# Causal mask and identity from a band read back from DRAM, with the head's steps in another order

## The chip, the cores and the metric

The kernel runs on one core of one Trainium2 chip. A core has five engines that run their own instruction streams side by side: TensorE (PE, matrix products; its weight loads are counted apart as PEld), VectorE (DVE), ScalarE (ACT), GpSimd (POOL) and SyncE (SP, which here only issues DMAs). Streams meet at semaphores. Data lies in DRAM, in SBUF (128 partitions) and in PSUM (the accumulators that PE writes).

The metric is device microseconds of one execution. Three runs of the kernel before took 962.62, 963.16 and 964.15 us (median 963.16).

## The reference, cut to what matters

```python
def _attn_ref(q, k, v, f_logit):             # 4 batches, 8 heads, 768 tokens, 48 features
    f = 1.0 / (1.0 + np.exp(-f_logit))
    state = zeros(B, H, D, D)
    for t in range(S):
        state = f[:, :, t, :, None] * state + einsum('bhd,bhe->bhde', k[:, :, t], v[:, :, t])
        y[:, :, t] = einsum('bhd,bhde->bhe', q[:, :, t], state)
    return y

def _moe_ref(x, w_in, w_out):                # 3072 tokens, 384 -> 2048 -> 384
    h = x @ w_in
    return (softplus(h) @ w_out)

def _moe2_ref(x, w_in, w_out):
    h = x @ w_in
    return (h * tanh(softplus(h))) @ w_out

def reference(**kwargs):
    x = heads_joined(_attn_ref(...))         # 3072 tokens x 384
    return _moe2_ref(x=_moe_ref(x=x, ...), ...)
```

The output is the second MLP's.

## The kernel before, in words

**Recurrence.** The 768 tokens of a batch are cut into 6 chunks of 128; a pair (chunk, batch) is a group, 24 in all, numbered by chunk first. Within a group the recurrence is written in closed form: running products of the decays (a scan on DVE, `a_scan`), their inverses (two ACT activations, `a_inv`), q and k scaled by them (`a_q`, `a_k` on DVE), all scores of a head pair at once on PE (`a_scores`), a causal mask on them (`a_mask`, two DVE products with `mask`, a 128x128 tile of ones on and above the diagonal), and the masked scores times v (`a_out`, `a_rest`). Eight heads of 48 features lie as four pairs. The outputs come feature first, in blocks of 48 rows, and must stand in x as three blocks of 128; so `a_out` makes the first rows of the pairs, `a_outed` copies them from PSUM on ACT (letter O), and `a_rest` puts them into place by a product with a 0/1 matrix `sel` (L407) and adds the other heads' rows (L411); `a_rested` copies the sum to x on ACT (letter R). `ident` is the 128x128 identity; `a_turn` needs it to transpose k for the states of the next chunk, and `sel` is filled with pieces of it.

**MLPs.** Layers 1 and 2 are cut into 6 blocks of 512 tokens by 16 blocks of 128 hidden features, 192 units in all. A unit is a product into the hidden block (L467 in the plain float32 units at the start, L481 later), the activation function (ACT and DVE), and a product out of it (L601, L611). The input weights arrive as float64 and are taken apart by integer operations on DVE and ACT: letters A (`whole_a`, DVE), B (`whole_b`, ACT L171) and C (`whole_c`, DVE L176 and L187) for a weight block.

**What sets the order around the change.** SP issues the first loads in the order of the table `LOADS`: f (decay logits), k (q and k together), v of a group, w a weight block. The steps ahead of the first unit are written out in the table `HEAD`, a letter and a group (or weight block) each, and are issued in that order on ACT, DVE, PE and SP; every engine runs its own share of them in the order of the table, so a step that waits holds up all steps of its engine behind it. Letters not named so far: e is exp of the logits on ACT, P and p add 1 on DVE or on ACT, s the scan, i the inverses, q and k the products, S the scores, m both masks, o and y the first rows of the outputs, b the rest of them, t T x X turns and states, h a number of matmuls without use (`warm`). After the head, units below 80 are ordered by the scheduler of the framework under hooks, and later ones by hand.

POOL makes `ident` and `mask` in the kernel before, by affine_select (through the helper `make_identity` at L742, and at L752), and fills `sel` from `ident` (L748); the matmuls of `warm` multiply `ident` by itself.

Of the kernel before, what the change touches and what calls it, by code (L numbers as in the profile page):

```python
# [8 lines left out]

F32 = mybir.dt.float32  # L10
F32R = mybir.dt.float32r
# [3 lines left out]
ALU = mybir.AluOpType  # L15
PSUM = bass.MemoryType.PSUM

B, H, S, D = 4, 8, 768, 48
C = 128
# [5 lines left out]
KD = DM // 128  # L25
N = B * C
R = 112
CAP = 2.0 ** 60
SAFE = 2.0 ** 40
# units are (layer, block of 512 tokens, block of 128 hidden features)  # L30
NAT = 8  # units of the first block whose products are plain float32
SPLITX = 5  # units before NAT at which its input is split
READY = 4  # weight blocks prepared before the first unit
AHEAD = 2  # units between the preparation of a weight block and its use
EARLY = 2  # units between its load and its preparation
LENT = (14, 12, 10, 8) * 3 + (14, 12, 14, 12)  # weight slots that stage a block of layer 1
SPAN = 8  # unit from which layer 2's weights are prepared
LEAD = 2  # units between their load and their preparation
HALVE = 1  # units between the split of a plain float32 block and its use
EVAC = 60  # L40
LAG = 4
LATE = 80  # from this unit on each engine's order is written out
PLACE = (12, 12, 15)
PLACE1 = (3, 3, 12)
HAND = {mybir.EngineType.Activation, mybir.EngineType.DVE, mybir.EngineType.PE}
# what is loaded first, in order: f, q and k ("k"), v of a group, weight block ("w")
LOADS = """
f0 k0 f1 k1 f2 f3 k2 v0 k3 v1 w0 v2 v3 w1 w2 w3 f4 k4 v4 f5 f6
"""
# the steps before the first unit: a letter of one() and a group or weight block  # L50
HEAD = """
h14 e0 P0 s0 e1 q0 P1 i0 s1 e2 k0 S0 q1 i1 P2 e3 k1 S1 p3 s2 i2 m0 o0 O0 h3 b0 q2 k2 S2 s3
i3 R0 m1 o1 O1 q3 k3 S3 m2 y2 A0 B0 O2 b1 R1 m3 y3 O3 b2 R2 C0 A1 B1 b3 R3 C1 t0 t1 A2 B2 T0
x0 T1 C2 X0 x1 t2 T2 X1 x2 A3 B3 t3 T3 X2 x3 C3 X3 l5 e4 p4 s4 i4 q4 k4 d4
"""

# [2 lines left out]
def recurrence__then__softplus_mish_mlps_kernel(  # L59
# [10 lines left out]
    nc = tc.nc  # L70
# [7 lines left out]
    dr_p = pool("dr", space=bass.MemoryType.DRAM, stack=ctx)  # L78
# [12 lines left out]
    ps_a = pool("ps_a", 1, PSUM)  # L91

    ident = const.tile([128, 128], F32, name="ident")
    mask = const.tile([128, C], F32, name="mask")
    cap = const.tile([128, NP, C + 1], F32, name="cap")
    tots = const.tile([128, NC * B, NP], F32, name="tots")
    rebias = keep.tile([128, 1], F32, name="rebias")
# [1 line left out]
    yd = dr_p.tile([B, DM, S], F32, name="yd")  # L99
    w2d = dr_p.tile([NF, 2, 128, 2 * DM], F32R, name="w2d")  # L100
    x2d = dr_p.tile([NC, 2, 128, KD, N], F32R, name="x2d")

    act, dve, pe = nc.scalar, nc.vector, nc.tensor

# [4 lines left out]
    n1 = len(tiles[1])  # L109
    tile_of = {c * B + b0 + j: k for k, (c, b0, nb) in enumerate(tiles[1]) for j in range(nb)}  # L110

    # ---------------------------------------------------------------- weights
    whi, wlo, w32 = {}, {}, {}

    raws = {}
# [17 lines left out]
        raws[layer, f] = raw, win  # L133

    def split_a(layer, f):
        """float64 -> its first 12 significant bits and what float32 keeps of the rest"""
        raw, win = raws[layer, f]
        s, m, sg = raw[:, :, 1], win[:, :, 1], raw[:, :, 0].bitcast(F32)
        act.activation(out=sg, in_=s, func=AF.Sign)
        dve.tensor_scalar(out=m, in0=m, scalar1=0x1FFFF, scalar2=None, op0=ALU.bitwise_and)  # L140
        dve.tensor_scalar(out=s, in0=s, scalar1=0x7FFFFE00, scalar2=None, op0=ALU.bitwise_and)
        act.activation(out=s, in_=s, func=AF.Relu, scale=8.0, bias=rebias)
# [14 lines left out]
        split_b(layer, f, hi, lo)  # L157

    def whole_a(f):
        """float64 -> float32"""  # L160
        raw, win = raws[1, f]
        s, m, e = raw[:, :, 1], win[:, :, 1], raw[:, :, 0]
        dve.tensor_scalar(out=e, in0=s, scalar1=0x7FF00000, scalar2=None, op0=ALU.bitwise_and)
        dve.tensor_scalar(
            out=m, in0=m, scalar1=0xFFFFFFF, scalar2=0x10000000,
            op0=ALU.bitwise_and, op1=ALU.bitwise_or,
        )
# [38 lines left out]
        whi[layer, f], wlo[layer, f] = w[:, 0], w[:, 1]  # L206
        return w[:, 0], w[:, 1]

    # -------------------------------------------------------------- attention
    G = {}  # L210

    def a_load_f(g):
# [229 lines left out]

    states = [const.tile([R, NP, D], F32, name=f"state{b}") for b in range(B)]

    # ------------------------------------------------------------------- MLPs
    xh, xl = {}, {}

    def split_x(key, kk):
# [194 lines left out]

        return [lambda c=c: part(c) for c in range(KD)]

    # --------------------------------------------------------------- schedule
    units = [(layer, k, f) for layer in (1, 2) for k in range(len(tiles[layer])) for f in range(NF)]
    index = {u: i for i, u in enumerate(units)}
    hooks = {}
# [6 lines left out]
            fn()  # L656

    def plan_prep(g, i):
        """the factors of group g over the units i-1 .. i+2"""
        at(i - 1, "act", a_exp, g)  # L660
        at(i, "dve1", a_scan, g)
        at(i, "act", a_inv, g)
        if g + 2 < NC * B:
            at(i, "act", a_load_f, g + 2)
        at(i + 1, "dve1", a_q, g)
        at(i + 2, "dve1", a_k, g)
        at(i + 2, "dve1", a_decay, g)

    def plan_attn(g, i):
        """the products of group g over the units i .. i+2"""  # L670
        at(i, "pe1", a_scores, g)
        at(i, "dve2", a_mask, g, 0)
        at(i, "dve2", a_mask, g, 1)
        at(i + 1, "pe1", a_turn, g)
        at(i + 1, "act", a_turned, g)
        at(i + 1, "pe2", a_out, g)
        at(i + 2, "act0", a_outed, g)
        if g < (NC - 1) * B:
            at(i + 2, "pe1", a_state, g)
            at(i + 2, "dve2", a_stated, g)  # L680
        if g + 2 < NC * B:
            at(i + 2, "dve2", a_load, g + 2)
# [53 lines left out]
        at(index[2, k, 0] - NF + 4, "act", load_x2, k)  # L736

    act.preload_act_table_set("natural_log_exp_and_others")
    for step in LOADS.split():
        what, g = step[0], int(step[1:])  # L740
        {"f": a_load_f, "k": a_load_qk, "v": a_load_v, "w": lambda f: load_w(1, f)}[what](g)
    make_identity(nc, ident)  # L742
    sel = st_p.tile([128, KD, 128], F32, tag="raw", name="sel")
    nc.gpsimd.memset(sel, 0.0)
    for p in range(KD):
        for i in range(2):
            o = 64 * i
            nc.gpsimd.tensor_copy(  # L748
                out=sel[:, p, o + D:o + 64], in_=ident[:, o + 16 * p:o + 16 * (p + 1)]
            )  # L750
    nc.gpsimd.memset(mask, 1.0)
    nc.gpsimd.affine_select(  # L752
        out=mask, in_=mask, compare_op=ALU.is_ge, fill=0.0, base=0,
        pattern=[[1, C]], channel_multiplier=-1,
    )
    dve.memset(cap[:, :, 0:C], CAP)
    dve.memset(cap[:, :, C:C + 1], 1.0)
    dve.memset(tots, 1.0)
# [3 lines left out]

    def warm(n):
        for z in range(n):
            pe.matmul(busy, ident, ident, start=True, stop=True)  # L765

    def one(step):
        fn, g = step[0], int(step[1:])
# [3 lines left out]
        else:  # L772
# [3 lines left out]
                "S": lambda g: a_scores(g, ps_o if g % 2 else ps_h), "o": a_out,  # L776
                "y": lambda g: a_out(g, ps_o), "O": a_outed, "t": lambda g: a_turn(g, ps_o),
                "T": a_turned, "x": lambda g: a_state(g, ps_o), "X": a_stated, "b": a_rest,
                "R": a_rested,
            }[fn](g)  # L780

    with tc.manual_schedule(engines=HAND | {mybir.EngineType.SP}):
# [30 lines left out]
    ]  # L813

    def late(i):
        """a unit of the second MLPs, each engine's instructions in the order written"""
        u = units[i] if i < n_units else None
        if u:
            m_h(u)
# [66 lines left out]
    assert not hooks, sorted(hooks)  # L886
    main.close()

    # ------------------------------------- decays too steep for the products
    redo = nc.values_load(  # L890
        slow[0:1, 0:1], min_val=0, max_val=1, skip_runtime_bounds_check_because="it is 0 or 1"
    )
# [181 lines left out]
```

## Time and profile before

| what | value |
|---|---|
| median of three runs | 963.16 us |
| span of the profiled execution (first to last instruction) | 960.3 us |
| what lies around the span, if that execution took as long as the median | 2.8 us |
| PE busy | 937.5 us, 98% of the span |
| DVE busy | 786.1 us, 82% |
| ACT busy | 739.0 us, 77% |
| POOL busy | 29.5 us, 3% |
| first matmul | 11.88 us |
| first product of the first unit (L467) | 32.63 us |

How to read it: the times are from the start of the span. A share of busy time is a mean over the whole span; the change lies in the first 35 us. The chain of waits is the list of the work that ended last, followed back from the end. A bracket at the end of a row of the timeline says how long the engine stood idle before that row and whose end it waited for. Line numbers are those of the kernel before; in the changed kernel the same lines are one higher up to L738 and seven higher from L756 on.

### The profile page before, as it was taken

The page shows a single profiled execution, that of the slowest core. Times are in us where ns is not written, and L with a number is a line of the kernel's source. Part 1 is how long each engine was busy: PE and PEld are TensorE (multiplying, and loading weights), DVE is VectorE, ACT ScalarE, POOL GpSimd, SP SyncE. Part 2 cuts the span into 40 slices and gives each one's busy share as a digit, 9 for nine tenths or more (in the row PEclk, how much of TensorE's full clock was granted, in tenths as well). Part 3 has the DMA queues.
Part 4 walks back from the last instruction along what each step waited for, and adds up shares of the span by engine and source line. Part 5 has one row for each costly group of instructions (what it writes and reads, how often), then busy time and mean ns, then how long its engine had stood idle before and what let it go on. Part 6 is the DMA issues. An engine that isn't in the chain of part 4 may idle for free.

```text
span 960.3 us, 13706 instructions
## 1 busy us (share of the span) xinstructions
PE 937.5 (98%) x4970; PEld 721.4 (75%) x4970; DVE 786.1 (82%) x1252; ACT 739.0 (77%) x1326; POOL 29.5 (3%) x84
## 2 busy tenths in 40 slices
PE   4999999999999999999999999999999999999997
PEld 4545767777777777877788888888888888888885
DVE  5999998988888888987677678787787887878875
ACT  4778896888788777866677678887788877887875
POOL 1000000000000000000003220000000000000000
PEclk9999999999999999999999999999999999999999
DMA  9799713354654746463008670100100201000001
GB/s 316 256 327 318 262 46 123 116 191 173 223 178 159 272 148 221 140 230 121 9 38 291 197 241 23 67 34 0 66 34 1 99 1 66 34 1 1 33 0 38
DMA packets 35117, 122.33 MB, mean 127 GB/s; under 512 B 4352, under 2 KB 7424, under 8 KB 35040
## 3 DMA queue, kind: packets, MB, share of 16 engines
q1 hardware_dynamic: 28704, 99.34, 29.8%
q0 software_dynamic: 6336, 22.02, 7.1%
q8 instruction: 41, 0.67, 0.3%
q14 instruction: 36, 0.29, 0.1%
HBM read 93.62 MB, written 26.74 MB: 125 GB/s over the span
## 4 chain that ended last, share of the span: by engine, by line
PE 93%; DVE 4%; issue 1%; ACT 1%; POOL 0%; ACTq 0%; POOLq 0%; DVEq 0%
PE po L611 39%; PE ps L481 39%; PE ps L389 3%; PE ps L397 3%; PE ps L322 2%; PE ps L467 2%; PE po L601 2%; PE ps L361 1%; PE ps L346 1%; PE busy L765 1%; DVE gg L256 0%; DVE a L335 0%; DVE w L147 0%; DVE d L518 0%; PE ps L407 0%
## 5 line engine op out<-in xcount | busy, mean ns | idle before, releaser
L481 PE MATMUL ps<-x,w 128*128 128x512 f32 x864 | 213.6, 392 | 0.0
L611 PE MATMUL po<-ghi,w 128*128 128x512 f32 x768 | 205.4, 398 | 0.0
L481 PEld LDWEIGHTS ps<-x,w 128*128 128x128 f32 x864 | 162.3, 188 | 36.3
L481 PE MATMUL ps<-xh,w 128*128 128x512 f32 x528 | 181.7, 399 | 2.1 <-DVE w L151 1.8
L611 PEld LDWEIGHTS po<-ghi,w 128*128 128x128 f32 x768 | 140.8, 188 | 31.1
L611 PE MATMUL po<-g,w 128*128 128x512 f32 x504 | 126.4, 395 | 0.0
L481 PEld LDWEIGHTS ps<-xh,w 128*128 128x128 f32 x528 | 98.8, 188 | 28.1 <-issue 3.4
L545 ACT ACTIVATE l<-d 128x512 f32<-128x512 f32 x96 | 60.7, 632 | 73.3 <-DVE d L541 73.3
L611 PE MATMUL po<-glo,w 128*128 128x512 f32 x384 | 112.4, 392 | 0.0
L611 PEld LDWEIGHTS po<-g,w 128*128 128x128 f32 x504 | 94.9, 188 | 21.9
L510 ACT ACTIVATE e<-ps 128x512 f32<-128x512 f32 x96 | 57.2, 596 | 70.1 <-PE ps L481 56.2
L481 PE MATMUL ps<-xl,w 128*128 128x512 f32 x264 | 103.1, 391 | 0.0
L501 DVE TENSOR_TENSOR glo<-l,ghi 128x512 fp32r<-128x512 f32 x128 | 87.8, 686 | 17.6 <-ACT ghi L496 16.7
L541 DVE TENSOR_SCALAR d<-ps 128x512 f32<-128x512 f32 x96 | 66.3, 691 | 37.3 <-PE ps L481 37.2
L555 DVE SCALAR_TENSOR_TENSOR l<-d,l 128x512 f32<-128x512 f32 x96 | 66.5, 692 | 33.1 <-ACT l L548 33.0
L496 ACT CAST ghi<-l 128x512 fp32r<-128x512 f32 x128 | 78.1, 610 | 14.4 <-DVE l L531 14.0
L518 DVE SCALAR_TENSOR_TENSOR d<-d,e 128x512 f32<-128x512 f32 x96 | 65.9, 687 | 26.5 <-ACT d L512 26.3
L611 PEld LDWEIGHTS po<-glo,w 128*128 128x128 f32 x384 | 72.1, 188 | 15.9
L578 DVE TENSOR_TENSOR l<-ps,l 128x512 f32<-128x512 f32 x96 | 66.4, 692 | 9.6 <-ACT l L575 0.9
L524 DVE TENSOR_TENSOR d<-l,d 128x512 f32<-128x512 f32 x96 | 65.9, 686 | 2.7
L570 DVE SCALAR_TENSOR_TENSOR l<-d,l 128x512 f32<-128x512 f32 x96 | 65.4, 682 | 0.0
L511 ACT ACTIVATE e<-e 128x512 f32<-128x512 f32 x96 | 60.7, 632 | 1.6
(107 smaller groups left out, 1306.0 us busy)
## 6 DMA issues: line engine op xcount, KB each, us to landing
raw<-in_w_dram SPq DMA_DIRECT2D x32, 768.0 KB, 6.2
w2d<-wo SPq DMA_DIRECT2D x32, 384.0 KB, 3.0
w<-w2d POOLq DMA_DIRECT2D x32, 384.0 KB, 3.9
raw<-in_w_dram SPq DMA_DIRECT2D x16, 767.9 KB, 10.3
win<-in_w_dram SPq DMA_DIRECT2D x16, 767.9 KB, 7.3
qk<-in_qkT_dram SPq DMA_DIRECT2D x22, 448.0 KB, 4.3
x2d<-o SPq DMA_DIRECT2D x12, 768.0 KB, 5.1
x<-x2d POOLq DMA_DIRECT2D x12, 768.0 KB, 5.8
```

What stands on the lines that cost most here:

```text
L481: pe.matmul(ps, w, r, start=(i == 0), stop=(i == len(steps) - 1))
L496: act.copy(out=t["hi"], in_=t["g"])
L501: dve.tensor_tensor(out=t["lo"], in0=t["g"], in1=t["hi"].bitcast(F32), op=ALU.subtract)
L511: act.activation(out=e, in_=e, func=AF.Exp, scale=-1.0)
L518: dve.scalar_tensor_tensor(out=d, in0=d, scalar=1.0, in1=t["e"], op0=ALU.subtract, op1=ALU.subtract)
L524: dve.tensor_tensor(out=d, in0=l, in1=d, op=ALU.subtract)
L541: dve.tensor_scalar(out=t["t"], in0=t["h"], scalar1=20.0, scalar2=None, op0=ALU.min)
L545: act.activation(out=t["l"], in_=t["t"], func=AF.Exp)
L555: dve.scalar_tensor_tensor(out=t["l"], in0=t["t"], scalar=-43.0, in1=t["l"], op0=ALU.max, op1=ALU.add)
L570: dve.scalar_tensor_tensor(out=t["l"], in0=t["t"], scalar=-1.0, in1=t["l"], op0=ALU.mult, op1=ALU.max)
L578: dve.tensor_tensor(out=t["l"], in0=t["h"], in1=t["l"], op=ALU.mult)
L611: pe.matmul(acc[c], w[layer, f][:, cols[c]], t[part], start=(f == 0 and part == "hi" and w is whi), stop=(f == NF - 1 and part == "lo"),)
```

## The change

`make_identity`, both affine_selects and POOL's six copies into `sel` go. In their place POOL fills a tile `step` (128 rows of 257 elements: zero, then 128 ones, then zeros) by two memsets, stores it to a DRAM tile `stepd` (128.5 KB), and loads `band` (128 x 129) from it with rows that begin 256 elements apart; since a stored row has 257, each row of the band is shifted by one against the row above. `band[:, 1:129]` is the mask, and the mask less `band[:, 0:128]` is the identity, which DVE computes in a new step n0; two ACT copies in the same step fill `sel`. The 14 passes of `warm` in front become 20, on `cap` (a tile that DVE fills at the start); the 3 later become 2. In `LOADS`, v0 goes ahead of f3 and v1 ahead of k3. In `HEAD`, the steps stand in another order.

```diff
 LOADS = """
-f0 k0 f1 k1 f2 f3 k2 v0 k3 v1 w0 v2 v3 w1 w2 w3 f4 k4 v4 f5 f6
+f0 k0 f1 k1 f2 v0 f3 k2 v1 k3 w0 v2 v3 w1 w2 w3 f4 k4 v4 f5 f6
 """
 HEAD = """
-h14 e0 P0 s0 e1 q0 P1 i0 s1 e2 k0 S0 q1 i1 P2 e3 k1 S1 p3 s2 i2 m0 o0 O0 h3 b0 q2 k2 S2 s3
-i3 R0 m1 o1 O1 q3 k3 S3 m2 y2 A0 B0 O2 b1 R1 m3 y3 O3 b2 R2 C0 A1 B1 b3 R3 C1 t0 t1 A2 B2 T0
+h20 e0 P0 s0 e1 q0 P1 i0 s1 e2 k0 S0 q1 i1 n0 p2 e3 p3 m0 k1 S1 o0 O0 h2 b0 R0 s2 i2 q2 m1 o1 O1 b1
+R1 k2 S2 s3 i3 q3 m2 y2 O2 b2 R2 k3 S3 A0 B0 m3 y3 O3 b3 R3 C0 A1 B1 C1 t0 t1 A2 B2 T0
 x0 T1 C2 X0 x1 t2 T2 X1 x2 A3 B3 t3 T3 X2 x3 C3 X3 l5 e4 p4 s4 i4 q4 k4 d4
 """
...
-    mask = const.tile([128, C], F32, name="mask")
+    band = const.tile([128, C + 1], F32, name="band")
+    mask = band[:, 1:C + 1]
...
+    stepd = dr_p.tile([128 * (2 * C + 1)], F32, name="stepd")
...
+    step = at1.tile([128, 2 * C + 1], F32, tag="kn", name="step")
+    nc.gpsimd.memset(step, 0.0)
+    nc.gpsimd.memset(step[:, 1:C + 1], 1.0)
+    nc.gpsimd.dma_start(out=stepd.rearrange("(s t) -> s t", s=128), in_=step)
+    nc.gpsimd.dma_start(
+        out=band, in_=stepd[0:256 * C].rearrange("(s t) -> s t", s=128)[:, 0:C + 1]
+    )
...
-    make_identity(nc, ident)
...
-    for p in range(KD):
+    def units_and_places(_):
+        dve.tensor_tensor(out=ident, in0=mask, in1=band[:, 0:C], op=ALU.subtract)
         for i in range(2):
             o = 64 * i
-            nc.gpsimd.tensor_copy(
-                out=sel[:, p, o + D:o + 64], in_=ident[:, o + 16 * p:o + 16 * (p + 1)]
+            act.copy(
+                out=sel[:, :, o + D:o + 64],
+                in_=ident[:, o:o + D].rearrange("s (p r) -> s p r", p=KD),
             )
-    nc.gpsimd.memset(mask, 1.0)
-    nc.gpsimd.affine_select(
...
-            pe.matmul(busy, ident, ident, start=True, stop=True)
+            pe.matmul(busy, cap[:, 0, 0:128], cap[:, 0, 0:128], start=True, stop=True)
...
-                "R": a_rested,
+                "R": a_rested, "n": units_and_places,
```

Three places show what the new table moves. First PE from its start (L322, in the changed kernel L323, are the scores; L389/L390 the first rows of the outputs; L407/L408 and L411/L412 the rest; `qk` and `qkv` are the tiles of groups 0, 1 and of 2, 3). Before:

```order
L322 MATMUL ps<-qk 128x128 x16
L389 MATMUL ps<-a,vt 64x128 x2
L765 MATMUL busy<-ident 128x128 x3
L407 MATMUL ps<-y_256,sel 128x128 x3
L411 MATMUL ps<-a,vt 48x128 x6
L322 MATMUL ps<-qkv 128x128 x8
L389 MATMUL ps<-a,vt 64x128 x2
L322 MATMUL ps<-qkv 128x128 x8
L389 MATMUL ps<-a,qkv 64x128 x2
L407 MATMUL ps<-y_256,sel 128x128 x3
```

And in the changed kernel, on the same engine and from the same point:

```order
L323 MATMUL ps<-qk 128x128 x16
L390 MATMUL ps<-a,vt 64x128 x2
L772 MATMUL busy<-cap 128x128 x2
L408 MATMUL ps<-y_254,sel 128x128 x3
L412 MATMUL ps<-a,vt 48x128 x6
L390 MATMUL ps<-a,vt 64x128 x2
L408 MATMUL ps<-y_254,sel 128x128 x3
L412 MATMUL ps<-a,vt 48x128 x6
L323 MATMUL ps<-qkv 128x128 x8
L390 MATMUL ps<-a,qkv 64x128 x2
L408 MATMUL ps<-y_254,sel 128x128 x3
```

The scores of group 2 (the first row on `qkv`) stand behind both output steps of group 1 now, and not ahead of them.

Second ACT, from the inverses of group 1 on (L279 and L280, in the changed kernel L280 and L281, are the two activations of an inverse, L424/L425 is O, L431/L432 is R, L241/L242 e and L244/L245 p). Before:

```order
L279 ACTIVATE f<-gg 112x4x128
L280 ACTIVATE f<-f 112x4x128
L241 ACTIVATE f<-f 112x516
L244 ACTIVATE f<-f 112x516
L279 ACTIVATE f<-gg 112x4x128
L280 ACTIVATE f<-f 112x4x128
L424 COPY y_256<-ps 128x128
L279 ACTIVATE f<-gg 112x4x128
L280 ACTIVATE f<-f 112x4x128
L431 COPY x<-ps 128x3x128
```

And the changed kernel's ACT from the same inverses on:

```order
L280 ACTIVATE f<-gg 112x4x128
L281 ACTIVATE f<-f 112x4x128
L758 COPY sel<-ident 128x3x16 x2
L245 ACTIVATE f<-f 112x516
L242 ACTIVATE f<-f 112x516
L245 ACTIVATE f<-f 112x516
L425 COPY y_254<-ps 128x128
L432 COPY x<-ps 128x3x128
L280 ACTIVATE f<-gg 112x4x128
L281 ACTIVATE f<-f 112x4x128
L425 COPY y_254<-ps 128x128
L432 COPY x<-ps 128x3x128
```

The copies into `sel` and group 2's add of 1 are new on ACT, and the inverses of group 2 stand behind O and R of group 0.

Third DVE, from the product q of group 1 (L286/L287) on; L292/L293 is a product k, L247 an add of 1, L256/L257 and L262/L263 a scan with its reciprocal, L335/L336 the masks. Before:

```order
L286 TENSOR_TENSOR qk<-qk,gg 112x512
L247 TENSOR_SCALAR f<-f 112x516
L292 TENSOR_TENSOR qk<-qk,f 112x512
L256 SCALAR_TENSOR_TENSOR gg<-f,cap 112x516
L262 RECIPROCAL tots<-gg 112x4
L335 TENSOR_TENSOR a<-ps,mask 128x512 x2
L286 TENSOR_TENSOR qkv<-qkv,gg 112x512
```

And the changed kernel's DVE from the same product on:

```order
L287 TENSOR_TENSOR qk<-qk,gg 112x512
L755 TENSOR_TENSOR ident<-band 128x128
L336 TENSOR_TENSOR a<-ps,band 128x512 x2
L293 TENSOR_TENSOR qk<-qk,f 112x512
L257 SCALAR_TENSOR_TENSOR gg<-f,cap 112x516
L263 RECIPROCAL tots<-gg 112x4
L287 TENSOR_TENSOR qkv<-qkv,gg 112x512
L336 TENSOR_TENSOR a<-ps,band 128x512 x2
```

The identity, which needs the band, and the masks of group 0 now stand ahead of k of group 1 and of the scan of group 2.

## Rows read from the trace of the kernel before

**Rows 1.** Page, shares by engine of the chain that ended last.

```profile
PE 93%; DVE 4%; issue 1%; ACT 1%; POOL 0%; ACTq 0%; POOLq 0%; DVEq 0%
```

**Rows 2.** Chain of waits, 0 to 60 us: start, length, what.

```profile
1.61 9.82 issue
...
18.53 1.29 DVE a L335 x2
...
42.62 0.86 DVE raw L176
...
51.54 1.12 PE po L601 x2
```

**Rows 3.** POOL's timeline: start, length, line, operation, idle before in brackets.

```profile
1.13 0.42 POOL L744 MEMSET sel<- 128x384 f32 x1
```

**Rows 4.** DVE's timeline, 0 to 34 us.

```profile
9.16 0.68 DVE L286 TENSOR_TENSOR qk<-qk,gg 112x512 f32<-112x512 f32 x1
...
18.53 1.29 DVE L335 TENSOR_TENSOR a<-ps,mask 128x512 f32<-128x512 f32 x2 [5.40 <-PE ps L322]
...
20.93 1.22 DVE L256 TENSOR_TENSOR_SCAN gg<-f,cap 112x516 f32<-112x516 f32 x1
...
22.29 1.26 DVE L335 TENSOR_TENSOR a<-ps,mask 128x512 f32<-128x512 f32 x2
...
31.68 0.96 DVE L176 SCALAR_TENSOR_TENSOR raw<-raw 128x768 int32<-128x768 int32 x1 [0.81 <-ACT raw L171]
```

**Rows 5.** DMA issues, 0 to 40 us: count, KB each, median us to landing.

```profile
f<-in_fT_dram SPq DMA_DIRECT2D x7, 225.8 KB, 4.1
...
qkv<-in_v_dram SPq DMA_DIRECT2D x2, 192.0 KB, 9.6
```

**Rows 6.** DMA issues of the whole span: the quickest store.

```profile
out_dram<-o SPq DMA_DIRECT2D x18, 256.0 KB, 2.1
```

**Rows 7.** POOL's load of w2d at 502.4 us, behind SP's two stores.

```profile
DMA to landing us min/median/max: 5.8/5.8/5.8
```

**Rows 8.** POOL's load of w2d at 527.0 us, alone.

```profile
DMA to landing us min/median/max: 3.5/3.5/3.5
```

**Rows 9.** PE's timeline, 0 to 34 us.

```profile
17.26 2.06 PE L322 MATMUL ps<-qk 48*128 48x128 f32 x32
...
23.65 0.44 PE L389 MATMUL ps<-a,vt 128*64 128x128 f32 x4
...
30.15 0.94 PE L407 MATMUL ps<-y,sel 128*128 128x128 f32 x6
31.02 0.86 PE L411 MATMUL ps<-a,qkv 128*48 128x128 f32 x12
...
32.63 1.90 PE L467 MATMUL ps<-x,w 128*128 128x512 f32 x4
```

**Rows 10.** ACT's timeline, 0 to 34 us.

```profile
12.94 0.63 ACT L279 ACTIVATE f<-gg 112x512 f32<-112x512 f32 x1 [0.80 <-DVE gg L256]
...
23.39 0.46 ACT L431 COPY x<-ps 128x384 f32<-128x384 f32 x1
24.16 0.27 ACT L424 COPY y<-ps 128x128 f32<-128x128 f32 x1 [0.31 <-PE ps L389]
...
30.64 1.01 ACT L171 ACTIVATE raw<-raw,rebias 128x768 int32<-128x768 int32 x1
```

**Rows 11.** Stretches: length; PE, PEld, DVE, ACT, POOL busy; PE clock, DMA share, GB/s.

```profile
40.00:50.00 10.00, 10.00 (x62) 4.82 (x62) 9.72 (x18) 9.14 (x18) 0.00 (x0) 1.00 1.02 342
60.00:80.00 20.00, 20.00 (x103) 9.72 (x103) 18.50 (x31) 14.45 (x25) 0.11 (x1) 1.00 1.00 337
2.00:4.00 2.00, 0.00 (x0) 0.00 (x0) 0.00 (x0) 0.41 (x2) 0.00 (x0) 1.00 1.00 313
```

**Rows 12.** PE's warm passes, 12.0 to 16.05 us.

```profile
11.88 4.42 PE L765 MATMUL busy<-ident 128*128 128x128 f32 x19 [11.88 <-POOL ident masks.py:199]
```

**Rows 13.** PE's warm passes, 16.3 to 17.0 us.

```profile
15.89 1.33 PE L765 MATMUL busy<-ident 128*128 128x128 f32 x9
```

More of the change, by code (lines that the diff above doesn't have):

```diff
@@ L7 @@
 from concourse._compat import with_exitstack
-from concourse.masks import make_identity
 F32 = mybir.dt.float32
@@ L741, in recurrence__then__softplus_mish_mlps_kernel @@
         {"f": a_load_f, "k": a_load_qk, "v": a_load_v, "w": lambda f: load_w(1, f)}[what](g)
-    make_identity(nc, ident)
     sel = st_p.tile([128, KD, 128], F32, tag="raw", name="sel")
     nc.gpsimd.memset(sel, 0.0)
-    for p in range(KD):
+    def units_and_places(_):
+        dve.tensor_tensor(out=ident, in0=mask, in1=band[:, 0:C], op=ALU.subtract)
         for i in range(2):
             o = 64 * i
-            nc.gpsimd.tensor_copy(
-                out=sel[:, p, o + D:o + 64], in_=ident[:, o + 16 * p:o + 16 * (p + 1)]
-            )
-    nc.gpsimd.memset(mask, 1.0)
-    nc.gpsimd.affine_select(
-        out=mask, in_=mask, compare_op=ALU.is_ge, fill=0.0, base=0,
-        pattern=[[1, C]], channel_multiplier=-1,
-    )
+            act.copy(
+                out=sel[:, :, o + D:o + 64],
+                in_=ident[:, o:o + D].rearrange("s (p r) -> s p r", p=KD),
+            )
     dve.memset(cap[:, :, 0:C], CAP)
```

## Prediction

> **What bounds the kernel now.** I read the chain of waits first. PE has 93% of it, DVE 4% and "issue" 1% [rows 1], so almost the whole span is matmuls in a row, and a change in the head counts only by what it shifts the start of that row. In order of time [rows 2] the chain begins with 9.82 us of issue: POOL stands until 11.43 in front of its first affine_select, and PE's first matmul, which reads the identity, comes at 11.88 [rows 12]. The first masks of DVE stand at 18.53, after 5.40 us in which DVE had nothing to do [rows 4]; the first unit's product starts on PE at 32.63 [rows 9]. From 42.62 the chain is on DVE until PE's L601 at 51.54 [rows 2]. The stretches say why: between 40 and 50 us DVE is busy for 9.72 of 10 us, while between 60 and 80 it is busy for 18.50 of 20, with PE full in both [rows 11]. So two engines have to come earlier if the end is to come earlier: PE at the first unit, and DVE at about 31 us, from where it works without a break up to 51.5.
>
> **What goes.** The 9.82 us of issue. All that needed POOL's identity or mask can now start when the band is there, and the scores as soon as k of group 0 is there. DVE's q of group 1 begins at 9.16 and takes 0.68 [rows 4], and the product k of group 0 is the one that ends as it begins, so the scores S0 can start near 9.3. They take half of 2.06 = 1.03 [rows 9], to 10.3. What is late next is the band, or those scores: no mask can begin before 10.3.
>
> **When the band comes.** POOL's memset of `sel` ends at 1.13 + 0.42 = 1.55 [rows 3]; one more memset, of 128 columns, follows, so I let the store begin at 1.8. Two DMAs come one after the other, since the load reads what the store wrote. No row shows such a transfer between 2 and 10 us, so it is bounded. From below: the quickest store of its kind takes 2.1 [rows 6], twice that makes 1.8 + 4.2 = 6.0, which is before the scores end and costs nothing. In the middle: POOL's load at 502.4, issued while two stores of SP were under way, took 5.8 us against 3.5 alone [rows 7, 8], 2.3 more. In the head the DMA engines are full (share 1.00 between 2 and 4 us [rows 11]), so I give each hop 2.1 + 2.3 = 4.4, near to the 4.1 median of SP's loads of f there [rows 5]: 1.8 + 8.8 = 10.6. From above: each hop takes as long as SP's loads that are queued behind all others, 9.6 [rows 5]: 1.8 + 19.2 = 21.0. I take 10.6, because the load at 502.4 is the only row with a POOL transfer beside a backlog of SP.
>
> The Trainium skill ("DMA: Bandwidth & Descriptors", section "Queues, rings and completion order") says that each DMA engine goes round between the queue rows that have work and changes at packet bounds. By it a small transfer on POOL's queue would hardly wait for SP's backlog, and the band would be in place before the scores end. The sum would then be that of a band in time, -1.0, 962.2, which lies within the main case below. Of this the trace shows only that SP's stores cost POOL's load 2.3 us [rows 7, 8].
>
> **The chain with the band at 10.2 or before.** Prices: two masks and two products lie between 18.53 and 20.93, and the first masks take 1.29, so I count 1.2 for a pair of masks and 0.6 for a product; scan and reciprocal 22.29 - 20.93 = 1.36 [rows 4]; o 0.44, b from 30.15 to 31.88, 1.73 [rows 9]; an inverse 2 x 0.63, O 0.27, R 0.46, B 1.01 [rows 10]. The identity is a product of 128 columns and not 512, 0.2. Then:
> m0 from 10.1 to 11.3, k1 to 12.0, S1 to 13.1, o0 to 13.6, O0 to 13.9, h2 and b0 to 15.7, R0 to 16.2. ACT holds the inverse i2 behind R0, so it ends at 17.5, while DVE has done s2, q2 and m1 by 15.1: it stands for 2.4 us until k2 (18.1), then s3 and q3 (20.1). PE holds S2 behind b1, so S2 ends at 20.7, m2 at 21.9, k3 at 22.6. S3 is behind b2 and ends at 25.5, m3 at 26.7, o3, O3, b3, R3 follow to 29.6, and the two turns to 30.2 on PE. The first unit starts at 30.2 and not at 32.63, 2.4 earlier. On DVE the second C, at 31.68 before [rows 4], needs B1, which stands behind R3 on ACT: 29.6 + 1.0, so 30.7, which is 1.0 earlier.
>
> So the 8 us that the head gains at its start are given back by three orders: i2 behind R0, S2 behind b1, S3 behind b2. Of the rest, DVE's 1.0 counts and PE's 2.4 does not, because the chain passes over DVE from 42.62 to 51.54 and DVE's work up to there is the same. Each us of the band beyond 10.2 moves all of this by 1 us: at 10.6 it is -1.0 + 0.4 = -0.6. A band at 11.2 makes it even, and beyond that each us is lost.
>
> **The other edits.** The copies into `sel` (two on ACT) and group 2's add of 1 (moved from DVE to ACT, 0.6) lie in ACT's time before O0 at 13.6, which has nothing else between the inverse of group 1 and there; without that cover they would cost their 1.2. The two POOL DMAs go ahead of nothing on SP. Moving v0 ahead of f3 puts 192 KB before 226 KB, some 0.6 us later for f3, whose scan stands behind k2 at 18.1; no cost. POOL's memsets of the v tiles now stand behind two issues, and are wanted by b0 only. The warm passes read a tile that DVE fills at the start, and need no POOL: zero on their own, see the clock below. The wait that is added is DVE's on the band; behind it are m0, k1 and s2, and by k1 also S1 on PE.
>
> **Sum.** The profiled execution has a span of 960.3; with 2.8 around it, taken from the median of 963.16, it stands at the median. 963.2 - 0.6 = 962.6.
>
> **The rivals.**
> *The band comes late* (slower). POOL's transfers stand in line behind what SP has already issued. If the store takes the 4.1 of the loads of f and the load the 9.6 of the loads of v [rows 5], the band is there at 15.5, 5.3 beyond 10.2: -1.0 + 5.3 = +4.3, 967.5. With both at 9.6 it is 21.0, +9.8, 973.0. For it: the engines are full all that time [rows 11], and a POOL load did lose 2.3 us to two stores [rows 7, 8]. Against it: that loss is a quarter of a backlog of the same size. It decides from a band at 13.1 on, where -1.0 + 2.9 passes +0.2%.
> *PE's whole lead carries* (faster). If the scheduler places the units' work on DVE so that PE's lead is not lost at 51.54, the end moves by the first unit's 2.4: 960.8; at a band of 10.6 by 2.0, 961.2. For it: between 60 and 80 us DVE has 1.5 us free in 20 [rows 11], and the order below unit 80 is made anew. Against it: DVE is busy 9.72 of 10 between 40 and 50 [rows 11] and its work can't shrink.
> *The TensorE clock* (slower). The passes at 11.88 take 4.42 for 19 records, 0.233 each, the later ones 1.33 for 9, 0.148 each [rows 12, 13], though the granted clock reads 1.00, the level of 2.4 GHz, even while PE does nothing [rows 11]. So the first passes after idle time ran at about half of what the later ones reach. With S1 and o0, b0 at twice their time, after PE's idle stretch from 10.3 to 12, the path gets 1.03 + 0.44 + 1.73 = 3.2 longer: 965.8. For it: the stretch is new. Against it: the passes and S0 run right up to it, while the passes of before had 11 us of idle time ahead of them.
>
> [...]
>
> **How the numbers follow.** The main case (band between 6 and 12, DVE sets the gain) has 0.45, with its own range of 962.0 (-1.2) to 964.2 (+1.0); the late band 0.26; PE's lead 0.21; the clock 0.08. The range goes from 960.6, just under PE's lead, to 971.0, which leaves out the late band's last part. A measurement of this kernel tells about 0.2% from no change, 1.93 us, so the bounds are 961.2 and 965.1. Faster: the greater part of PE's lead, and little of the main case, 0.22. Slower: the late band and the clock, 0.33. The main case and some of the rest is the same, 0.45.
>
> **What would show it.** In the profile after: DVE's identity step, and the idle time before it ended by the DMA of the band, gives the band's arrival; 10.6 right, above 13 the late rival. The inverse of group 2 after R of group 0 on ACT, and DVE idle for some 2.4 before k of group 2 with the ACT as releaser; S2 and S3 on PE right behind L412, with DVE waiting for them before m2 and m3. The first unit's L468 at 30.6 and the second L177 at 31.1. Then a longer wait of PE at L602 than before, and from there both kernels' chains side by side, 0.6 apart. I am wrong if the band is early and L468 starts later than 32.6, or if PE passes L602 more than 1.5 us earlier than before.

## The result, and the profile after

The changed kernel takes 972.25 us (median; 969.85 to 974.46) against 963.28 of the kernel before on the same chip: ratio of the two 1.0088, 95% interval 1.0069 to 1.0107. It is slower by 9 us, and lies 1.25 us above the predicted range. The ratios in this document leave out two executions far from all others, 1856 us of the first run below and 5239 us of the kernel before. The profiled execution took 969.85 with a span of 968.1, 7.8 more than the span before.

The head tells most of it. DVE's timeline of the kernel after (start, length, line, operation; the bracket is idle time and what ended it), which answers to [rows 4]:

```profile
15.79 0.29 DVE L755 TENSOR_TENSOR ident<-band 128x128 f32<-128x128 f32 x1 [5.69 <-DMA band<-stepd]
16.00 1.28 DVE L336 TENSOR_TENSOR a<-ps,band 128x512 f32<-128x512 f32 x2
...
25.14 0.69 DVE L293 TENSOR_TENSOR qkv<-qkv,f 112x512 f32<-112x512 f32 x1 [3.81 <-ACT f L281]
...
28.16 1.29 DVE L336 TENSOR_TENSOR a<-ps,band 128x512 f32<-128x512 f32 x2 [0.40 <-PE ps L323]
...
33.14 1.29 DVE L336 TENSOR_TENSOR a<-ps,band 128x512 f32<-128x512 f32 x2 [2.15 <-PE ps L323]
...
39.55 0.96 DVE L177 SCALAR_TENSOR_TENSOR raw<-raw 128x768 int32<-128x768 int32 x1 [2.32 <-ACT raw L172]
```

The first masks start at 16.0, 2.5 us earlier than the 18.53 of [rows 4]. Behind them DVE stands four times, for the inverse of group 2, for the scores of groups 2 and 3, and for B; its second C (L177 of weight block 1) comes at 39.55 where it came at 31.68, 7.9 later, as much as the end lost (7.8). The two DMA issues of the band, from the profile after, 0 to 40 us (KB, us to landing):

```profile
stepd<-step POOLq DMA_DIRECT2D x1, 128.5 KB, 6.6
band<-stepd POOLq DMA_DIRECT2D x1, 64.5 KB, 6.8
```

PE's timeline after, which answers to [rows 9]:

```profile
9.54 1.16 PE L323 MATMUL ps<-qk 48*128 48x128 f32 x16 [1.69 <-DVE qk L293]
17.93 2.08 PE L323 MATMUL ps<-qk 48*128 48x128 f32 x16 [7.22 <-DVE qk L293]
...
31.95 1.16 PE L323 MATMUL ps<-qkv 48*128 48x128 f32 x16
...
35.27 1.37 PE L408 MATMUL ps<-y,sel 128*128 128x128 f32 x6 [0.35 <-ACT y L425]
36.57 1.52 PE L412 MATMUL ps<-a,qkv 128*48 128x128 f32 x12
38.02 1.45 PE L347 MATMUL ps<-ident,qk 112*128 112x112 f32 x8
39.31 2.75 PE L468 MATMUL ps<-x,w 128*128 128x512 f32 x6
```

And its stretches, with the columns of [rows 11]:

```profile
8.00:10.00 2.00, 0.46 (x8) 0.46 (x10) 1.97 (x4) 0.72 (x3) 0.56 (x1) 1.00 1.10 293
...
12.00:16.00 4.00, 0.00 (x0) 0.00 (x0) 0.21 (x2) 0.00 (x0) 0.00 (x0) 0.50 1.03 330
...
18.00:20.00 2.00, 2.00 (x18) 1.78 (x19) 1.78 (x3) 0.26 (x1) 0.00 (x0) 0.50 1.10 424
...
22.00:24.00 2.00, 1.61 (x21) 1.25 (x20) 0.00 (x0) 0.56 (x2) 0.00 (x0) 1.00 1.04 427
...
28.00:30.00 2.00, 0.99 (x8) 0.38 (x4) 1.84 (x4) 0.75 (x3) 0.00 (x0) 1.00 0.98 402
...
36.00:38.00 2.00, 2.00 (x15) 1.43 (x14) 1.23 (x3) 0.00 (x0) 0.00 (x0) 0.50 0.00 0
```

S0 runs in 1.16 us at 9.54. Then PE idles for 7.22 us, the granted clock goes from 1.00 to 0.50 (from 2.4 to 1.2 GHz), and the same 16 records of group 1 take 2.08. PE is idle again for most of the time from 33 to 34 us, and from 36 to 38 the clock is at 0.50 once more: L412, the same work, takes 1.52 instead of 0.86 [rows 9]. The first unit starts at 39.31, 6.7 us later than before.

So three things are on the table: the late band, the new order, and the clock.

### The profile page after: what moved, and what is told of

It is laid out like the page before. It is cut to its first block, busy times and chain, and to the rows that moved or that the text cites. A ratio compares the mean times of both kernels' runs of the same rounds, so it can differ in the third digit from the quotient of the medians.

```text
span 968.1 us, 13730 instructions
## 1 busy us (share of the span) xinstructions
PE 942.8 (97%) x4980; PEld 724.6 (75%) x4980; DVE 786.4 (81%) x1252; ACT 741.1 (77%) x1329; POOL 28.7 (3%) x78
## 4 chain that ended last, share of the span: by engine, by line
PE 93%; DVE 3%; DMA 1%; ACT 1%; issue 1%; POOL 0%; ACTq 0%; DVEq 0%; POOLq 0%
PE po L612 40%; PE ps L482 39%; PE ps L390 3%; PE ps L398 3%; PE ps L323 3%; PE ps L468 2%; PE po L602 1%; PE ps L362 1%; PE ps L347 1%; DMA band<-stepd 1%; DMA stepd<-step 1%; DVE a L336 0%; PE ps L408 0%; PE ps L412 0%; DVE w L148 0%
## 5 line engine op out<-in xcount | busy, mean ns | idle before, releaser
L497 ACT CAST ghi<-l 128x512 fp32r<-128x512 f32 x128 | 78.0, 609 | 17.6 <-DVE l L532 17.2
L612 PEld LDWEIGHTS po<-glo,w 128*128 128x128 f32 x384 | 72.1, 188 | 15.7
## 6 DMA issues: line engine op xcount, KB each, us to landing
raw<-in_w_dram SPq DMA_DIRECT2D x16, 767.9 KB, 10.2
```

The lines of the kernel that those rows point to most:

```text
L497: act.copy(out=t["hi"], in_=t["g"])
L612: pe.matmul(acc[c], w[layer, f][:, cols[c]], t[part], start=(f == 0 and part == "hi" and w is whi), stop=(f == NF - 1 and part == "lo"),)
```

## The experiments

**The old order with the new band.** The table of before, with 20 passes and n0:

```diff
-h20 e0 P0 s0 e1 q0 P1 i0 s1 e2 k0 S0 q1 i1 n0 p2 e3 p3 m0 k1 S1 o0 O0 h2 b0 R0 s2 i2 q2 ...
+h20 e0 P0 s0 e1 q0 P1 i0 s1 e2 k0 S0 q1 i1 P2 e3 k1 S1 p3 s2 i2 n0 m0 o0 O0 h3 b0 q2 k2 S2 s3 ...
```

> The changed kernel with the kernel before's table of steps, n0 put right ahead of m0 and the first passes 20 instead of 14; band, loads and passes on cap as changed. In the changed kernel the first masks start at 16.0, 2.5 us earlier than before, and yet the first unit starts 6.7 us later. Theory A (the order of the steps is the cause: the inverse of group 2 behind R0, the scores of groups 2 and 3 behind the outputs): the band still lands at about 15.8, the masks start at 16, the first unit at 30 to 31, time 960 to 962. Rival B (the late band is the cause, whatever the order): the first unit still starts after 36 and the time stays over 968.

Measured: 964.04, ratio to before 1.0002 (0.9993 to 1.0012). DVE's first masks in this run:

```profile
16.53 1.28 DVE L336 TENSOR_TENSOR a<-ps,band 128x512 f32<-128x512 f32 x2
```

And on PE the outputs behind them and the first unit:

```profile
17.27 1.35 PE L390 MATMUL ps<-a,vt 128*64 128x128 f32 x4 [3.48 <-DVE a L336]
...
21.40 1.52 PE L412 MATMUL ps<-a,vt 128*48 128x128 f32 x12
...
32.27 4.47 PE L468 MATMUL ps<-x,w 128*128 128x512 f32 x10
```

With the band as late as in the changed kernel, and with its loads and passes, the loss is gone: 8.2 of the 9 us come with the new order. That does not make the late band free. The kernel before with passes on cap (961.19, below) starts its masks at 14.48, 2.05 earlier than here, and is 2.9 us faster; the passes on cap and the late band nearly cancel in this run (loads and the number of passes differ too between the two, and no run took them apart). The expected gain did not come, though the masks start 2 us earlier than before: PE stood 3.48 us ahead of L390, the granted clock is 0.50 from 14 to 22 us, L412 takes 1.52 instead of 0.86 [rows 9], and from the masks to the first unit it is 15.7 us instead of 14.1.

**The new order without the band.** Identity, mask and `sel` by POOL again:

```diff
...
-    nc.gpsimd.dma_start(out=band, in_=stepd[...])
...
-    dve.tensor_tensor(out=ident, in0=mask, in1=band[:, 0:C], op=ALU.subtract)
+    make_identity(nc, ident)
...
+    nc.gpsimd.affine_select(out=mask, in_=mask, ...)
```

> The changed order, loads and passes on cap, but identity, mask and the six copies made by GpSimd as before (no band, no n0). Theory A (order): the mask is there at about 13.8, 2 us before the changed kernel's band, the rest follows in the changed order, first unit at about 37, time 968 to 971. Rival B (the late band is the cause): with the band gone the first unit comes by 32.6 or earlier, time 963 or less.

Measured: 971.4, ratio 1.0063 (1.0038 to 1.0088). The masks start at 13.65 and the first unit at 41.43, later than in the changed kernel although the mask is earlier; the granted clock is 0.50 from 26 to 34 us, where the changed kernel had 1.00. Theory A is borne out in that the order loses without any band. Its first unit at 37 is not.

**One transfer and not two.**

```diff
...
-    nc.gpsimd.dma_start(out=stepd..., in_=step)
-    nc.gpsimd.dma_start(out=band, in_=stepd[...])
+    row = step[0:1, C - 1:2 * C]
+    nc.gpsimd.dma_start(
+        out=band, in_=bass.AP(row.tensor, row.offset, [list(row.ap[0]), [-1, 128], [1, C + 1]]))
```

> The changed kernel, but the band comes by one DMA from SBUF to SBUF, from one row of 256 elements read with overlap; no store to DRAM, no second transfer. Theory A, with the band's lateness counted one to one: the DMA takes about 6.7, as each of the two did, so the band lands at 8.5 to 9.5, the masks wait for the scores at 10.7 instead of 16.0, and the first unit starts 5 us earlier than in the changed kernel, at about 34; time 965 to 968, still slower than before. Rival C (TensorE's lower clock after its idle stretch from 10.7 to 17.9 is the main cause): with the idle stretch gone the first unit comes 5 us plus at least 3 us earlier, time under 964.

Measured: 971.05, ratio 1.0057 (1.0033 to 1.0080), single executions from 964.89 to 973.23. The transfer takes 5.3 us, the masks start at 11.91 and wait only for the scores, and the first unit still starts at 39.68. Both numbers of the expectation are missed. Stretches of this run:

```profile
16.00:20.00 4.00, 4.00 (x26) 3.44 (x28) 1.24 (x2) 0.27 (x1) 0.00 (x0) 0.52 1.02 402
24.00:28.00 4.00, 3.22 (x24) 2.36 (x20) 2.22 (x5) 1.64 (x3) 0.00 (x0) 0.50 1.01 416
28.00:32.00 4.00, 3.64 (x22) 2.67 (x22) 1.18 (x3) 0.38 (x2) 0.00 (x0) 0.50 0.94 361
```

The clock is at its lower level from 16 to 20, and again from 24 to 32; in that second stretch the changed kernel had 1.00. Executions with a mean granted clock of 0.992 to 0.994 took 964.89 to 967.31, those with 0.987 to 0.991 took 971.05 to 973.23: the clock looked like the missing part.

**The kernel before with passes on cap, one edit.**

```diff
-            pe.matmul(busy, ident, ident, start=True, stop=True)
+            pe.matmul(busy, cap[:, 0, 0:128], cap[:, 0, 0:128], start=True, stop=True)
```

> The kernel before with one edit: the passes of warm multiply cap by itself and not the identity. S0 then starts at 9.3 instead of 17.3, the first masks at 13.9, when GpSimd's mask is there, instead of 18.5. Theory A: the head and the end move by 4.6, 958 to 959. Rival C (clock): TensorE idles between the scores and the masks, its clock falls, and half of it or more is lost, 961 to 963.

Measured: 961.19, ratio 0.9979 (0.9970 to 0.9988). The masks start at 14.48 and the first unit at 29.67, 3 us earlier than before. The scores S0 and S1 take 4.10 for the work that takes 2.06 in [rows 9], with the granted clock at 0.50 from 10 to 20 us:

```profile
10.32 4.10 PE L322 MATMUL ps<-qk 48*128 48x128 f32 x32 [3.05 <-DVE qk L292]
```

The rival's size was right.

**The changed kernel with its idle time on PE filled.** The clock and the order are taken apart by keeping the order:

```diff
-k0 S0 q1 ... o1 O1 b1 / R1 k2 S2 s3 ... k3 S3
+k0 S0 h30 q1 ... o1 O1 h6 b1 / R1 k2 S2 H3 s3 ... k3 S3 H3        (H: passes into a later buffer)
```

> The changed kernel with more passes on cap where PE idled: 30 after S0, 6 behind O1 ahead of b1, 3 behind S2 and 3 behind S3. Theory C (the clock falls after each idle stretch and part of the loss is S1, o0, b0 and later b3 and the turns at half rate): granted clock 1.00 through the head, the scores of group 1 take 1.1 and not 2.1, first unit 2 to 3 us earlier, time 968 to 970 with a spread of runs as narrow as before's. Theory A alone (order, waits): the clock does not matter, time as the changed kernel, 971 to 973.

Measured: 970.77, ratio 1.0068 (1.0055 to 1.0082). The band came at 17.2 in this run, 1.5 later than in the changed kernel's profile, so the comparison runs from the masks on. The granted clock is 0.50 from 12 to 14 us and 0.67 from 14 to 16, under the passes themselves, and 1.00 from 16 to 52. DVE's first masks:

```profile
17.46 1.28 DVE L336 TENSOR_TENSOR a<-ps,band 128x512 f32<-128x512 f32 x2
```

And on PE the passes, the scores of group 1 and the first unit:

```profile
11.91 8.57 PE L780 MATMUL busy<-cap 128*128 128x128 f32 x60
20.41 1.16 PE L323 MATMUL ps<-qk 48*128 48x128 f32 x16
...
38.50 5.57 PE L468 MATMUL ps<-x,w 128*128 128x512 f32 x12
```

From the masks to the first unit it is 21.0 us, and 23.3 in the changed kernel, against 14.1 before (18.53 to 32.63). The 2.3 between the first two is less than the clock's whole price: the passes run until S1 begins, 2.95 us behind the start of the masks, where it begins 1.93 behind it in the changed kernel, so 1.0 of the 21.0 is the passes'.

The time does not show this gain clearly: 1.0068 has an interval that overlaps the changed kernel's (1.0069 to 1.0107), and the profiled execution took 971.68, with a span 1.9 longer than that of the changed kernel's. One wait behind the head is new in it. PE's waits of this run (in total, times, longest):

```profile
PE po L602 <- DVE g L532: 4.7, 1, 4.7
```

It stands ahead of 55.81, and the changed kernel has none there. DVE reaches its first L532 at 54.99 in this run and at 48.91 in the changed kernel; the scheduler put DVE's steps behind the head into another order. So an edit in the head can also change the time by what the scheduler makes of the units.

**Only the inverses first.**

```diff
-S1 o0 O0 h2 b0 R0 s2 i2 q2 m1 o1 O1 b1 / R1 k2 S2 s3 i3 q3
+S1 s2 i2 o0 O0 h2 b0 R0 q2 m1 o1 O1 b1 / k2 S2 s3 i3 R1 q3
```

> The changed kernel with one move: the scan and the inverse of group 2 (and of group 3) ahead of the copies O0 and R0 (R1) in the table, so that ACT makes the inverse before the outputs. Theory A in its first part (the inverse behind R0 holds DVE for 3.8 us): the stretch of DVE ahead of k2 goes, but S2 still waits for b1 on PE, so only some 1 of the 3.8 shows at the first unit: time 970 to 972. If the inverse alone were the cause: 967 to 968.

Measured: 974.2, ratio 1.0106 (1.0091 to 1.0122). DVE's wait for the inverse is gone, as expected, but the wait for the scores of group 2 grows from 0.40 to 3.59, and the first unit starts at 40.37:

```profile
27.66 1.29 DVE L336 TENSOR_TENSOR a<-ps,band 128x512 f32<-128x512 f32 x2 [3.59 <-PE ps L323]
```

So the inverse alone is not the bound: S2 behind b1 is next in line at once. Its interval overlaps the changed kernel's, so that it is slower still is not shown. The granted clock was 0.75 between 28 and 32 us, where the changed kernel had 1.00. No run took this apart.

**Inverses and scores first.**

```diff
-S1 o0 O0 h2 b0 R0 s2 i2 q2 m1 o1 O1 b1 / R1 k2 S2 s3 i3 q3 m2 y2 O2 b2 R2 k3 S3
+S1 s2 i2 o0 O0 h2 b0 q2 m1 k2 S2 s3 i3 R0 o1 O1 b1 / R1 q3 m2 k3 S3 y2 O2 b2 R2
```

> The changed kernel with the inverses of groups 2 and 3 ahead of R0 and the scores S2 and S3 ahead of the output steps o1, b1 and y2, b2; band, n0, passes as changed. Theory A (the three orders are the cause): the masks of groups 2 and 3 no longer wait for output steps, DVE runs through from 16.0, first unit at 30.5 to 32, time 961.5 to 964. Rival B (late band): still over 968.

Measured: 966.53, ratio 1.0030 (1.0019 to 1.0041): 5.7 of the 9 us are back. The first unit starts at 35.71, not at 31, and the time lies between what the two theories gave. Part of what is left stands on DVE:

```profile
25.65 1.29 DVE L336 TENSOR_TENSOR a<-ps,band 128x512 f32<-128x512 f32 x2 [1.41 <-PE ps L323]
...
33.05 0.96 DVE L177 SCALAR_TENSOR_TENSOR raw<-raw 128x768 int32<-128x768 int32 x1 [2.57 <-ACT raw L172]
```

C0 waits for B0, which ACT has behind R2; in the kernel before B0 stands ahead of O2. This fourth order was not in the prediction. The granted clock was 0.50 from 14 to 24 us here too; no run had this order with the clock kept.

**The kernel before, passes on cap, PE kept busy.**

```diff
-h14 e0 ... k1 S1 p3
+h34 e0 ... k1 S1 h12 p3        (and the passes on cap)
```

> The kernel before with the passes on cap, as in the run with that one edit, and more of them: 34 instead of 14 in front, 12 behind S1. Theory C (the clock): the granted clock stays at 1.00, S0 and S1 take 2.1 instead of 4.1, the steps up to b0 run at full rate, first unit at 28 to 28.5 instead of 29.7; time 959.5 to 960.8 against 961.2 with the one edit. Rival (DVE sets the end, what PE gains in the head is lost): 961.2 as with the one edit.

Measured: 959.71, ratio 0.9961 (0.9947 to 0.9975). The clock stays at 1.00:

```profile
12.00:16.00 4.00, 4.00 (x52) 3.88 (x49) 2.82 (x6) 1.74 (x3) 1.54 (x9) 1.00 1.03 337
```

S0 and S1 take 2.06, the first unit starts at 28.64. Theory C is right in its direction and its size, though the interval overlaps a little that of the run with one edit (0.9970 to 0.9988).

**The changed order, early band, PE kept busy.** The one transfer and passes (8 behind S0, 6, 3 and 3 as above).

> The changed order with the band by one transfer, and passes on cap where PE idled: 8 after S0, 6 behind O1, 3 behind S2 and 3 behind S3. With the clock kept the changed order took 21.0 us from the first masks to the first unit (17.5 to 38.5), where the order of before took 14.1. Theory (band, order and clock add up): masks at 11.9 and the first unit at 33 instead of 39.7, granted clock 1.00, time 963.5 to 966, and the runs spread no more than 2 us where the run without passes spread over 8. Rival (the clock has no part; the order's waits fill whatever the band gives): first unit at 38 to 40, time 970 to 972.

Measured: 964.56, ratio 1.0002 (0.9992 to 1.0012), executions from 962.14 to 965.70. DVE's first masks:

```profile
11.48 1.29 DVE L335 TENSOR_TENSOR a<-ps,band 128x512 f32<-128x512 f32 x2 [0.45 <-PE ps L322]
```

And PE's scores of group 3 and its first unit:

```profile
25.70 1.16 PE L322 MATMUL ps<-qkv 48*128 48x128 f32 x16
...
31.50 2.75 PE L467 MATMUL ps<-x,w 128*128 128x512 f32 x6
```

The granted clock is 1.00 throughout the head. From the masks to the first unit it is 20.0 us, so the lower clock costs the changed kernel 3.3 of its 23.3. R of group 0 on ACT tells where, first in the changed kernel, then here:

```profile
23.44 0.48 ACT L432 COPY x<-ps 128x384 f32<-128x384 f32 x1 [2.47 <-PE ps L412]
```

```profile
17.18 0.48 ACT L431 COPY x<-ps 128x384 f32<-128x384 f32 x1 [1.89 <-PE ps L411]
```

It starts 7.44 us behind the masks there and 5.70 here, 1.7 apart; the scores of group 3 (31.95 and 25.70) are 1.7 apart as well, and the first unit 3.3. So about half of the loss lies in S1 to b0, and the other half behind S3, where the clock falls for the second time.

Against the same kernel without passes that is 6.5 us (971.05), by passes that compute nothing (5.3 by the two ratios, whose intervals lie apart). The executions spread over 3.6 us, not the 2 that were expected. Against the changed kernel with passes and the late band, the masks are 17.46 - 11.48 = 6.0 us earlier, the first unit 7.0 (1.0 of it by the fewer passes ahead of S1), and the time 970.77 - 964.56 = 6.2 lower. So each us of the band counts in full up to the first unit, once the clock is kept; the times agree with that, but the two profiled spans lie 9.0 apart, since the 4.7 us wait of the run above is missing here.

**The old order, early band, PE kept busy.** The table of before with 28 passes in front, 8 behind S1, group 2's add on ACT and n0 next behind q1 on DVE; loads as changed.

> The order of before, band by one transfer, passes on cap that keep PE busy (28 in front, 8 behind S1, 3 behind o0), group 2's add of 1 on ScalarE, identity by VectorE right after q of group 1. Against the kernel before with passes on cap and filled gaps (959.7) VectorE no longer waits 1.1 us for GpSimd's mask. Theory: first masks at 13.2 to 13.6 instead of 14.5, first unit at 27.5 to 28, time 958.5 to 959.5. Rival (what the head gains is lost later on): 959.7 or more.

Measured: 959.90, ratio 0.9953 (0.9940 to 0.9967). The masks come at 13.83 and the first unit at 27.96, 0.7 earlier than with POOL's mask, and the time is the same as 959.71. PE's waits of this run (in total, times, longest):

```profile
PE ps L481 <- DVE w L151: 1.8, 1, 1.8
```

The rival's number came: what the head gains is lost later on. Where is not shown. The 1.8 us wait for a weight block, at 127 us, is missing in the run with 959.71, but the kernel before has the same line.

**SyncE held until the band is there.** One transfer that reads the band stands on SP's queue behind f2 and v0:

```diff
+        if step == "f2":
+            nc.sync.dma_start(out=stepd[0:C].rearrange("(s t) -> s t", s=1), in_=band[0:1, 0:C])
```

> The changed kernel, with one more transfer on SyncE's queue behind f2 and v0 that reads the band, so that SyncE issues no further load until the band is there. If the band is late because its two transfers share the DMA engines with SyncE's loads: the first lands at 7 to 9 as before, the second, alone on the engines, takes 2 to 3 us and not 6.8, band at 10 to 11. If a transfer by GpSimd takes 6.6 us by itself: band at 15 to 16 still. The time itself is worse, since the loads come later, and is not the question.

Measured: one execution of 967.33. The DMA issues of its first 14 us:

```profile
stepd<-step POOLq DMA_DIRECT2D x1, 128.5 KB, 5.8
band<-stepd POOLq DMA_DIRECT2D x1, 64.5 KB, 2.0
```

The second transfer is issued at 8.2 and lands at 10.2. It is the same 64.5 KB that took 6.8 beside SP's loads; the DMA engines' share is 0.34 between 8.5 and 9 us and 0.04 in the half us behind it. So the second transfer is late because it shares the DMA engines with SP's loads, and not because a transfer of POOL is slow. The first still took 5.8, beside the loads that SP had issued before. The time was expected to be worse and was lower than any of the changed kernel's four, with the masks at 11.58 and SP's later loads issued 7 us late; it is one execution, and nothing more was drawn from it.

All of it in one table, in us (masks: start of the first masks; unit: start of the first unit; second C: start of DVE's second L176 or L177; all three from the profiled execution; time: the median):

| kernel | masks | unit | masks to unit | second C | time |
|---|---|---|---|---|---|
| before | 18.53 | 32.63 | 14.1 | 31.68 | 963.3 |
| changed | 16.00 | 39.31 | 23.3 | 39.55 | 972.3 |
| old order, late band | 16.53 | 32.27 | 15.7 | 31.32 | 964.0 |
| changed order, POOL's mask | 13.65 | 41.43 | 27.8 | 41.40 | 971.4 |
| changed order, one transfer | 11.91 | 39.68 | 27.8 | 39.66 | 971.1 |
| before, passes on cap | 14.48 | 29.67 | 15.2 | 28.74 | 961.2 |
| changed, clock kept | 17.46 | 38.50 | 21.0 | 39.20 | 970.8 |
| changed, inverses first | 16.20 | 40.37 | 24.2 | 40.47 | 974.2 |
| changed, inverses and scores first | 16.37 | 35.71 | 19.3 | 37.09 | 966.5 |
| old order, passes on cap, clock kept | 14.51 | 28.64 | 14.1 | 27.70 | 959.7 |
| changed order, one transfer, clock kept | 11.48 | 31.50 | 20.0 | 32.20 | 964.6 |
| old order, one transfer, clock kept | 13.83 | 27.96 | 14.1 | 27.01 | 959.9 |
| changed, SP held | 11.58 | 34.06 | 22.5 | 34.77 | 967.3 (one execution) |

From the second C to the end of the span it is 928.6 us in the kernel before and in the changed one, and 928.0 to 932.6 in the others. The runs come from several chips, on which the kernel before took 963.3 to 964.1. So the columns of the head can be compared closely, and differences of a few us between times can come from behind the head.

## Why the prediction was wrong

- **The scores at 9.3.** Right: 9.54, and the masks wait for the band.
- **The band at 10.6.** This is the first step that failed. The sum gave each transfer 4.4 us, from a load that ran beside two stores of SP. They took 6.6 and 6.8, the first issued at 2.1 and not at 1.8, with 0.3 between them, and the band landed at 15.8. The late rival's 15.5 is near to that by luck: v's 9.6 was too long for the second transfer, and f's 4.1 too short for the first. The run with SP held shows what the excess of the second is: 4.8 of the 6.8 is the queue beside it. That of the first was not taken apart. The masks came 5.9 us behind the 10.1 of the sum. (The sum could not have had 10.1: by its own terms the scores end at 10.3, and the identity's 0.2 lies behind the band. The slip is 0.3.)
- **The clock.** This is the second step that failed: the sum had the passes at nothing "on their own" and the clock only as a rival of 0.08, as though it and the late band's 0.26 excluded each other. The late band left PE idle from 10.7 to 17.9, and the clock fell in that stretch. It cost 3.3 from the masks to the first unit (23.3 against 20.0 with the clock kept). That the rival had 3.2 is luck: it put all of it on S1, o0 and b0, where 1.7 was lost, and had no second fall behind S3, where the other 1.6 was. Nor do its two rows give half the rate (0.148 against 0.233 is 0.64); S0 and S1, 1.16 against 2.08, come nearer to it.
- **Either alone would have failed it.** With one transfer the band is there by 6.9 (issued at 1.62, 5.3 to landing), well within the 6 to 12 of the main case, and the masks start at 11.9. Yet the time is 971.05 and the first unit starts at 39.68; an early band with a first unit later than 32.6 is what the prediction had named as a sign of being wrong. The four kernels of the changed order, as ratios to the kernel before:

  | | clock low | clock kept |
  |---|---|---|
  | late band | 1.0088 | 1.0068 |
  | early band | 1.0057 | 1.0002 |

  Only both together bring the time back. The early band did not keep the clock by itself: there it was low in two longer stretches, from 16 to 20 and from 24 to 32. Why it fell there and not in the changed kernel is not settled; the rows show only that PE had idle time ahead of each fall.
- **The chain of the new order.** Right, for a clock that stays. It gave 20.1 us from the masks to the first unit; with the clock kept it was 20.0, and 21.0 where 1.0 was the passes'. At the masks' 11.48 it gives -1.0 + 1.4 = +0.4, and that run had a ratio of 1.0002. The three orders that it named are real: with all three of them undone 5.7 us came back. It left out that B0 behind R2 holds C0.
- **DVE sets the gain, PE's lead does not.** Consistent with the changed kernel: the second C came 7.9 later and the end 7.8, the first unit only 6.7. The longer wait of PE at L602 that was to show it did not come; PE waits 0.9 there before, and has no such wait in the changed kernel.

Put together, from the sum's own -1.0: 5.9 for the masks and 3.3 for the clock make +8.2, 971.4 us, which lies among the executions of the changed kernel.

The queue rule of the Trainium skill that the prediction cited ("DMA: Bandwidth & Descriptors", section "Queues, rings and completion order") was read there to mean that a small transfer hardly waits. Here it waited 4.8 us of 6.8, so that reading was wrong for a transfer beside a deep backlog; turns between queues may well be taken, but they did not keep 64.5 KB short.

The better kernels follow from the parts. The passes on cap, which the change contains, are worth having by themselves (0.9979), and with more of them, so that the clock stays, probably more so (0.9961; the intervals overlap a little). The band adds nothing to that that could be measured, as one transfer, and the new order loses.

## What to carry to other kernels

Cases that share a cause are not alternatives: if an input comes late, ask at once what the engine that waits for it will do to its own clock, and add the two. When an order is written by hand, put what feeds the next group (inverse, scores) ahead of what drains the last one (outputs, copies) on every engine that both pass; undoing it on one engine only moves the wait to the next. Matmuls without use are worth a try wherever TensorE waits in a chain of dependent steps: with the early band they gave 6.5 us to the new order, to the old order some 1.5 (intervals that overlap a little), and with the late band nothing clear, since they stood 1.0 us in the way of S1 and the units behind the head came in another order. And compare the head's own rows as well as the time, since behind the head something else may have moved.

## What the runs showed of the hardware that was not expected

A small DMA beside SP's loads had a price far above what it costs alone: 64.5 KB from DRAM took 6.8 us in the changed kernel and 2.0 with SP held. The store of 128.5 KB took 6.6, and 64.5 KB from SBUF to SBUF 5.3, beside the loads. The three differ in kind as well as in size, so what part the size has is not shown.

The granted clock fell more than once in a chain of dependent steps: in the changed kernel after 7.22 us of idle time on PE and again behind the idle time at 33 us; in the run with one transfer it was low from 16 to 20 and from 24 to 32. With that order and band the executions ran from 964.89 to 973.23, and from 962.14 to 965.70 with the idle time filled. That a low clock scatters times is not general here: the run with the inverses first had one too, and its four executions lie within 1.7 us.
